# A new order for every engine: planner slots, distance and step in a kernel of a Fourier half and a state-space half

## The chip, the cores and the metric

The kernel runs on one core of a Trainium2 chip. Five engines work side by side: TensorE (PE; its weight loads are listed apart as PEld), VectorE (DVE), ScalarE (ACT), GpSimd (POOL) and SyncE (SP), which here only issues transfers. The metric is the device time of one execution in microseconds (us); lower is better.

## The reference

Two independent layers, whose outputs stand side by side. All values are float32.

```
# A: Fourier mixing, x is 2048 x 512
a = x @ dft_hid_re.T ;  b = x @ dft_hid_im.T
y = dft_seq_re @ a - dft_seq_im @ b

# B: a diagonal state-space layer, u is 2048 x 512, 128 states per channel
dt = exp(log_dt);  A = -exp(log_A_real) + 1j * A_imag
P  = exp((A * dt)[:, :, None] * arange(2048))
K  = 2 * real(sum over the states of C * dt * P)        # one filter of 2048 taps per channel
y  = irfft(rfft(u, 4096) * rfft(K, 4096))[:2048] + u * D_skip

out = concatenate([A, B])
```

## The kernel before

**The Fourier half** (class `Fnet`) multiplies by the sequence matrix first and by the hidden one afterwards. It works in twelve groups, eight of sixteen tiles ("s") and four of eight tiles ("p", which reads the sums of the s groups back from memory). Each float32 tile is split into a rounded part `hi` (ACT, L231) and the rest `lo` (DVE, L236), and one product is three matmuls (L380): hi times hi, hi times lo, lo times hi. Of the s tiles, those in `SOFTS` get their `lo` without DVE: two accumulating transfers from GpSimd's queue do it (L329, L334). The matmuls of one tile for one of four output columns are one request of 0.683 us to TensorE; they are the stream that TensorE works on whenever nothing else is due (urgency 5).

**The state-space half** (class `Ssm`) has these stages:
- `setup` and `setup_rest`: exponentials (`exp`, L505) and parameters (`params`, L561), once for the first 128 columns and once for the other 384.
- Sixteen chunks of 32 channels. `seed_args` (L654) makes angles and moduli, mostly on ACT; `seeds` their products; `tables1` and `tables2` build tables of powers by repeated complex multiplication on DVE (L623 `prod`, L632 `t`, L639, L646, L652).
- `taps` (L818): 128 short matmuls per chunk give the filter's taps. `stage1_k` (L867): the first step of the filter's transform, per two chunks, stored to `xk`.
- `stage1_u` (L922): the same for the input, in eight parts.
- Four quarters of the channels, each in four parts: loads of both spectra (L999), `product` (matmuls L1046, pointwise products on DVE L1030 and L1032, matmuls L1073), a store to `zs` (L1097), and then two `inverse` (L1167) or, for the last two quarters, `inverse2` (additions on DVE L1136 and L1138, matmuls L1145, output).

**The order is planned on the host.** Instructions are issued to each engine in the order in which a small simulation (class `Plan`) finishes choosing them; semaphores keep the data right whatever the order. A stage is a generator that yields requests: an engine, a price, perhaps an urgency of its own, and for TensorE the number of instructions. `Plan.run` (L171) takes the request with the smallest `key` (L149): first the step of time in which it could start, in steps of `GRAIN`; within one step the urgency, smaller first; then the start itself. All instructions that the code issues after a yield, up to the next one, have that place in the order, whatever engine they are for.

`Plan.step` (L103) moves a request later than its process's last one: by `HOP` where the engine changes, and by `RESULT` where a DVE operation follows a DVE operation whose result it needs (those that are marked `*APART` do not need it). Prices are `act(cols)` and `dve(cols, rate)`, (66 + cols/rate)/960 us for DVE. A request to TensorE also bears the planner's model of instruction fetching, in blocks of 256.

Urgencies: splits 0 (3 when the stream is ahead), seeds, taps, products of the first quarters and stores 1, tables 2 and 2.2, third-quarter products 3 (`LATE`), last-quarter products 1 (`LAST`), inverses of the last two quarters 2 (`AFTER`), the stream 5.

In several places the yields do not match the instructions behind them: `exp` asks for DVE where an ACT operation follows, `seed_args` asks for a DVE slot with no instruction behind it, and `params` issues some operations without a slot.

Of the kernel before, what the change touches and what calls it, by code (L numbers as in the profile page):

```python
# [51 lines left out]
    return [np.ascontiguousarray(a.astype(np.float32)) for a in (f1u, f1k, w2, ia, ib, ib2)]  # L52


HOP, RESULT, LATENCY = 0.3, 0.15, 3.3
STREAM = 5
GRAIN = 0.05
BLOCK, ASKS, LASTS = 256, 110, 400
ASKED, APART_BY, COMES = 2.0, 3.8, 2.4
APART = None, True  # L60
LATE = 1, 1, 3, 1
AFTER = 2
LAST = 1


# [24 lines left out]
class Plan:  # L90
# [12 lines left out]
    def step(self, p, value):  # L103
        self.now = p[0]
        while True:
            try:
                r = p[3].send(value)
            except StopIteration:
                return
            value = None  # L110
            if isinstance(r, Event):
                if r.time is None:
                    r.waiting.append(p)
                    return
                p[0] = max(p[0], r.time)
            elif isinstance(r, Sem):
                if not r.free:
                    r.waiting.append(p)
                    return
                p[0] = max(p[0], r.free.pop(0))  # L120
            else:
                if r[0] != p[5]:
                    p[0] += HOP
                elif r[0] == "dve" and len(r) < 4:
                    p[0] += RESULT
                p[4], p[5] = r, r[0]
                self.ready.append(p)
                return
            self.now = p[0]
# [19 lines left out]
    def key(self, p):  # L149
        engine, _, *urgency = p[4]  # L150
        start = max(p[0], self.free.get(engine, 0.0))
        if engine == "pe":
            start += self.fetched(p[4], start)[0]
        return int(start / GRAIN), urgency[0]() if urgency and urgency[0] else p[1], start, p[2]

# [34 lines left out]
def act(cols):  # L190
    return 0.09 + cols * 0.00085


def dve(cols, rate=1.0):
    return (66 + cols / rate) / 960
# [6 lines left out]
class Fnet:  # L202
# [117 lines left out]
                self.plan.spawn(self.load(src, None, self.m, i, self.m_ev[i]), urgency)  # L320

    def soft(self, i):
        return i[0] == "s" and (2 * i[1] + i[2], i[3]) in SOFTS

    def load_soft(self, src, i):

        hi, lo = (self.pool.tile([128, DM], F32R, name=m, bufs=DEPTH) for m in ("hi", "lo"))
        yield "pool", ISSUE
        self.nc.gpsimd.dma_start(hi, src)  # L329
        yield "dma", load(256)  # L330
        yield "act", act(512)
        self.nc.scalar.activation(lo, hi.bitcast(F32), AF.Copy, scale=-1.0)  # L332
        yield "pool", ISSUE
        self.nc.gpsimd.dma_start(lo, src, accum_op=OP.add)  # L334
# [106 lines left out]
class Ssm:  # L441
# [63 lines left out]
    def exp(self, x, k, f, p):  # L505

        n = math.prod(x.shape[1:])
        a, v = self.nc.scalar, self.nc.vector
        yield "dve", dve(n, 2)
        v.tensor_scalar(x, x, -87.0, 88.0, op0=OP.max, op1=OP.min)  # L510
        yield "dve", dve(n, 2)
        v.tensor_scalar(k, x, 1.0 / math.log(2.0), RND, op0=OP.mult, op1=OP.add)
        yield "dve", dve(n, 2)
        v.tensor_scalar(k, k, RND, None, op0=OP.subtract)
        yield "dve", dve(n)
        v.scalar_tensor_tensor(f, k, -LN2_HI, x, op0=OP.mult, op1=OP.add)
        yield "dve", dve(n)
        v.scalar_tensor_tensor(f, k, -LN2_LO, f, op0=OP.mult, op1=OP.add)
        yield "dve", dve(n, 2)
        a.activation(p, f, AF.Copy, scale=EXP[0])  # L520
        for c in EXP[1:]:
            yield "dve", dve(n)
            v.scalar_tensor_tensor(p, p, c, f, op0=OP.add, op1=OP.mult)
        yield "dve", dve(n)
        yield "dve", dve(n, 2)
        a.activation(f.bitcast(I32), k, AF.Copy, scale=2.0 ** 23, bias=127.0 * 2.0 ** 23)
        yield "dve", dve(n)
        v.scalar_tensor_tensor(x, p, 1.0, f, op0=OP.add, op1=OP.mult)
# [32 lines left out]
    def params(self, par, alpha, dt, k):  # L561

        a, v = self.nc.scalar, self.nc.vector
        n = par.shape[2]
        yield "dve", dve(n), *APART
        v.tensor_tensor(par[:, 0], alpha, dt, op=OP.mult)
        yield "dve", dve(n), *APART
        v.scalar_tensor_tensor(par[:, 1], par[:, 1], 1.0 / (2 * math.pi), dt, op0=OP.mult, op1=OP.mult)

        a.activation(k, par[:, 1], AF.Copy, scale=-1.0, bias=RND)  # L570
        yield "dve", dve(n), *APART
        v.tensor_tensor(par[:, 2], par[:, 2], dt, op=OP.mult)
        yield "dve", dve(n), *APART
        v.scalar_tensor_tensor(par[:, 3], par[:, 3], -1.0, dt, op0=OP.mult, op1=OP.mult)
        v.scalar_tensor_tensor(par[:, 1], k, RND, par[:, 1], op0=OP.subtract, op1=OP.add)
        v.tensor_scalar(par[:, 1], par[:, 1], 0.5, -0.5, op0=OP.min, op1=OP.max)

    def setup(self):
# [75 lines left out]
    def seed_args(self, ck, box, ev):  # L654

        a, v = self.nc.scalar, self.nc.vector
        if CHUNK * ck >= FIRST:
            yield from self.load_par(ck)
        par = self.par[ck]
        yield self.res  # L660
        s = self.tab.tile([128, 3, 11, CHUNK], F32, name="seed")
        args = s[:, 0:3:2]
        e, k, r = (s[:, n] for n in range(3))
        n = 11 * CHUNK
        yield "act", act(2 * n) + 4 * act(0)
        a.activation(args[:, :, 0], par[:, 0:2], AF.Copy)
        for j in (1, 2, 4, 8):
            a.activation(args[:, :, j:min(2 * j, 11)], args[:, :, 0:min(j, 11 - j)], AF.Copy, scale=2.0 ** j)
        yield "act", act(n)
        a.activation(k[:, 1:], r[:, 1:], AF.Copy, scale=-1.0, bias=RND)  # L670
        yield "dve", dve(n)
        v.scalar_tensor_tensor(r[:, 1:], k[:, 1:], RND, r[:, 1:], op0=OP.subtract, op1=OP.add)
        yield "dve", dve(n, 2)
        yield "act", act(n)
        a.activation(k, r, AF.Abs)
        yield "act", act(n) + 1.3
        a.activation(e, e, AF.Exp, scale=-1.0)
        yield "act", act(6 * CHUNK) + 1.4
        a.activation(r[:, 0:6], r[:, 0:6], AF.Sin, scale=TWO_PI)
        yield "act", act(5 * CHUNK)  # L680
        a.activation(r[:, 6:11], r[:, 6:11], AF.Sin, scale=-TWO_PI)
        yield "act", act(n)
        a.activation(k, k, AF.Sin, scale=-TWO_PI, bias=self.halfpi)
        box.append(s)
        self.plan.set(ev)
# [417 lines left out]
    def inverses(self, h):  # L1103
# [5 lines left out]
        for i in range(2):  # L1109
            yield b.zls  # L1110
            self.plan.spawn((self.inverse2 if h >= HALVED else self.inverse)(b, h, i, 16), 1 if h < 2 else AFTER)

# [67 lines left out]
CHUNK, FIRST, JOIN = 32, 128, 0  # L1180
HALVED = 2
RAWS, DEPTH, STAGED, AHEAD = 7, 4, 4, 3
ISSUE = 1.0
SOFTS = {(g, k) for g in range(1, 8) for k in (3, 7, 11, 15)}
BATCH = 2


# [72 lines left out]
```

## Time and profile before

| | |
|---|---|
| median of 3 runs | 576.67 us (574.18 to 576.96) |
| profiled execution | 576.01 us |
| its span, from the first to the last instruction | 574.2 us |
| granted TensorE clock, mean | 0.999 |
| PE busy / weight loads | 566.7 us (99%) / 432.7 us (75%) |
| DVE busy | 518.5 us (90%) |
| ACT busy | 374.9 us (65%) |
| DMA | 133.70 MB, 233 GB/s |

The span is what the trace covers; the time of the execution is 1.8 us longer. A matmul's row is longer than the time until the next matmul starts, since they are pipelined, so a busy share of 99% says that TensorE nearly always has something in flight, not that it can do no more. Waits are the idle time of an engine before an instruction, with the event that ended it. The chain that ended last is followed back from the last instruction through what released each step.

### The profile page before, as it was taken

The page shows a single profiled execution, that of the slowest core. Times are in us where ns is not written, and L with a number is a line of the kernel's source. Part 1 is how long each engine was busy: PE and PEld are TensorE (multiplying, and loading weights), DVE is VectorE, ACT ScalarE, POOL GpSimd, SP SyncE. Part 2 cuts the span into 40 slices and gives each one's busy share as a digit, 9 for nine tenths or more (in the row PEclk, how much of TensorE's full clock was granted, in tenths as well). Part 3 has the DMA queues.
Part 4 walks back from the last instruction along what each step waited for, and adds up shares of the span by engine and source line. Part 5 has one row for each costly group of instructions (what it writes and reads, how often), then busy time and mean ns, then how long its engine had stood idle before and what let it go on. Part 6 is the DMA issues. An engine that isn't in the chain of part 4 may idle for free.

```text
span 574.2 us, 15643 instructions
## 1 busy us (share of the span) xinstructions
PE 566.7 (99%) x6278; PEld 432.7 (75%) x6278; DVE 518.5 (90%) x909; ACT 374.9 (65%) x734; POOL 40.3 (7%) x60
## 2 busy tenths in 40 slices
PE   8999999999999999999999999999999999999997
PEld 6877777788877777778787777777687778776685
DVE  6999999999999999999999999999999999447732
ACT  5789766673778495858669586845588845355623
POOL 0000101100110000100101001001100000000000
PEclk9999999999999999999999999999999999999999
DMA  7999999987459767867697888569998896599994
GB/s 247 329 358 274 289 285 283 274 281 196 134 148 223 210 184 227 202 164 236 181 250 198 222 206 259 134 164 278 276 299 227 226 298 230 125 281 270 276 228 147
DMA packets 147976, 133.70 MB, mean 233 GB/s; under 512 B 47296, under 2 KB 107328, under 8 KB 147648
## 3 DMA queue, kind: packets, MB, share of 16 engines
q1 hardware_dynamic: 138976, 115.54, 67.1%
q0 software_dynamic: 8064, 14.68, 12.8%
q10 hardware_dynamic: 864, 2.49, 1.7%
q8 instruction: 49, 0.80, 0.6%
q14 instruction: 23, 0.19, 0.1%
HBM read 89.95 MB, written 42.73 MB: 231 GB/s over the span
## 4 chain that ended last, share of the span: by engine, by line
PE 88%; DVE 7%; issue 2%; ACT 1%; DMA 1%; DVEq 0%
PE acc L380 69%; PE f L1046 5%; PE f L818 5%; PE f L1073 3%; DVE prod L623 2%; DVE t L632 2%; PE f L867 1%; DVE lo L236 1%; PE f L1167 1%; PE f L922 1%; PE f L1145 1%; DMA out_yb<-zl 1%; DMA raw<-in_sT 1%; DVE zl L934 0%; DVE t L652 0%
## 5 line engine op out<-in xcount | busy, mean ns | idle before, releaser
L380 PE MATMUL acc<-hi,x_hi 128*128 128x512 f32 x640 | 258.2, 403 | 0.1
L380 PE MATMUL acc<-lo,x_hi 128*128 128x512 f32 x640 | 250.3, 391 | 0.0
L380 PE MATMUL acc<-hi,x_lo 128*128 128x512 f32 x640 | 249.7, 390 | 0.0
L623 DVE TENSOR_TENSOR prod<-t,cs 128x1024 f32<-128x1024 f32 (+4 forms) x192 | 163.5, 870 | 1.8 <-ACT t L740 0.6
L380 PEld LDWEIGHTS acc<-hi,x_hi 128*128 128x128 f32 x640 | 120.3, 188 | 49.0 <-issue 23.0
L380 PEld LDWEIGHTS acc<-hi,x_lo 128*128 128x128 f32 x640 | 120.4, 188 | 26.0
L380 PEld LDWEIGHTS acc<-lo,x_hi 128*128 128x128 f32 x640 | 120.5, 188 | 23.1 <-DVE lo L236 0.2
L231 ACT ACTIVATE hi<-raw 128x512 fp32r<-128x512 f32 x132 | 82.8, 629 | 71.5 <-PE acc L380 56.2
L236 DVE TENSOR_TENSOR lo<-raw,hi 128x512 fp32r<-128x512 f32 x132 | 90.6, 688 | 25.3 <-ACT hi L231 25.0
L632 DVE TENSOR_TENSOR t<-prod 128x512 f32<-128x512 f32 (+4 forms) x192 | 94.6, 515 | 1.0
L639 ACT ACTIVATE square<-t 128x256 f32<-128x256 f32 (+1 forms) x64 | 36.8, 575 | 26.3 <-DVE t L632 24.4
L334 POOL DMA_DIRECT2D lo<-in_sT x28 | 24.3, 869 | 206.9 <-ACT lo L332 64.4
L1025 ACT ACTIVATE uk<-f 128x1024 f32<-128x1024 f32 x32 | 31.1, 1018 | 10.8 <-PE f L1046 9.0
L401 ACT ACTIVATE y<-acc 128x512 f32<-128x512 f32 x47 | 28.0, 595 | 12.8 <-PE acc L380 12.7
L818 PEld LDWEIGHTS f<-t,t 128*32 128x32 f32 x2048 | 29.5, 110 | 6.8 <-issue 4.8
L818 PE MATMUL f<-t,t 128*32 128x64 f32 x2048 | 32.2, 220 | 0.9 <-issue 0.8
L329 POOL DMA_DIRECT2D hi<-in_sT x28 | 15.8, 566 | 193.8 <-PE acc L380 135.5
L1030 DVE TENSOR_TENSOR z<-uk 128x512 f32<-128x512 f32 x32 | 22.0, 687 | 4.4 <-ACT uk L1025 2.9
L1088 ACT ACTIVATE z<-f 128x512 f32<-128x512 f32 x32 | 17.7, 593 | 12.0 <-PE f L1073 12.0
L652 DVE TENSOR_TENSOR t<-square 128x128 f32<-128x128 f32 (+1 forms) x64 | 25.0, 390 | 0.0
L1046 PE MATMUL f<-xt,w 64*32 64x256 f32 x768 | 23.5, 379 | 0.0
L1032 DVE TENSOR_TENSOR uk<-uk 128x512 f32<-128x512 f32 x32 | 22.1, 691 | 0.9
(104 smaller groups left out, 497.8 us busy)
## 6 DMA issues: line engine op xcount, KB each, us to landing
raw<-in_sT SPq DMA_DIRECT2D x99, 256.0 KB, 5.2
p<-y SPq DMA_DIRECT2D x32, 256.0 KB, 3.7
xk<-xk_sb SPq DMA_DIRECT2D x32, 256.0 KB, 5.2
zs<-z SPq DMA_DIRECT2D x32, 256.0 KB, 3.8
raw<-p SPq DMA_DIRECT2D x32, 256.0 KB, 4.6
hi<-in_sT POOLq DMA_DIRECT2D x28, 256.0 KB, 4.7
lo<-in_sT POOLq DMA_DIRECT2D x28, 256.0 KB, 5.0
xt<-xu SPq DMA_DIRECT2D x24, 256.0 KB, 4.6
```

Source lines behind the costliest of these rows:

```text
L231: self.nc.scalar.activation(hi, src, AF.Copy)
L236: self.nc.vector.tensor_tensor(lo, src, hi.bitcast(F32), op=OP.subtract)
L334: self.nc.gpsimd.dma_start(lo, src, accum_op=OP.add)
L380: nc.tensor.matmul(acc[d], l[:, cols], r, start=k == 0 and n == 0, stop=k == len(items) - 1 and n == 2)
L401: self.nc.scalar.activation(y, ps, AF.Copy, scale=-1.0 if g[2] == 1 else 1.0)
L623: self.nc.vector.tensor_tensor(p.rearrange("p k d c m -> p k (d c) m"), src.rearrange("p d c l -> p (d c) l")[:, None, :, rows].to_broadca ...
L632: self.nc.vector.tensor_tensor(dst[:, :, :, rows], p[:, 0], p[:, 1, :, ::-1], op=OP.add)
L639: self.nc.scalar.activation(sq, t[:, :, :, m // 2:m], AF.Square)
L652: self.nc.vector.tensor_tensor(t[:, :, 0, m:2 * m:2], box[0][:, :, 0], box[0][:, :, 1], op=OP.subtract)
L818: nc.tensor.matmul(ps[32 * j:32 * j + 32, i], t1[:, d, c], t2[:, d, c], start=c == 0, stop=c == 1, tile_position=(0, 32 * j))
L1025: a.activation(uk[:, r].rearrange("p g c n d -> p g (c n d)"), p, AF.Copy)
L1046: nc.tensor.matmul(got[r][1][32 * xx:32 * xx + 32, g, 256 * c:256 * c + 256], self.w2[rows, 2 * q + r, xx, 32 * c:32 * c + 32], xt[rows].r ...
```

## The change

Only the planner's numbers and the slots that the stages ask for are changed. No operation, tile, buffer or transfer is added or taken away; all engines and queues get the same instructions in an order planned anew.

- `RESULT` 0.15 to 0.2, `GRAIN` 0.05 to 0.1, `AFTER` 2 to 1.
- A new `SLACK` of 0.1 us on top of `HOP` where a process goes from another engine to TensorE.
- `exp`: the two ACT operations get ACT slots, where there were one and two DVE slots.
- `params`: the ACT operation and two DVE operations get slots of their own.
- `seed_args`: two slots are shorter by 32 columns, and a DVE slot without an operation goes.
- `SOFTS` is written out as a list of 28 pairs, and `soft` asks for `SOFT`, groups 1 to 7, too.

```diff
-HOP, RESULT, LATENCY = 0.3, 0.15, 3.3
+HOP, RESULT, LATENCY = 0.3, 0.2, 3.3
 STREAM = 5
-GRAIN = 0.05
+SLACK = 0.1
+GRAIN = 0.1
...
-AFTER = 2
+AFTER = 1
...
                 if r[0] != p[5]:
-                    p[0] += HOP
+                    p[0] += HOP + (SLACK if r[0] == "pe" else 0.0)
...
     def soft(self, i):
-        return i[0] == "s" and (2 * i[1] + i[2], i[3]) in SOFTS
+        return i[0] == "s" and 2 * i[1] + i[2] in SOFT and (2 * i[1] + i[2], i[3]) in SOFTS
...
         v.scalar_tensor_tensor(f, k, -LN2_LO, f, op0=OP.mult, op1=OP.add)
-        yield "dve", dve(n, 2)
+        yield "act", act(n)
         a.activation(p, f, AF.Copy, scale=EXP[0])
...
-        yield "dve", dve(n)
-        yield "dve", dve(n, 2)
+        yield "act", act(n)
         a.activation(f.bitcast(I32), k, AF.Copy, scale=2.0 ** 23, bias=127.0 * 2.0 ** 23)
...
+        yield "act", act(n)
         a.activation(k, par[:, 1], AF.Copy, scale=-1.0, bias=RND)
...
+        yield "dve", dve(n), *APART
         v.scalar_tensor_tensor(par[:, 1], k, RND, par[:, 1], op0=OP.subtract, op1=OP.add)
+        yield "dve", dve(n, 2)
         v.tensor_scalar(par[:, 1], par[:, 1], 0.5, -0.5, op0=OP.min, op1=OP.max)
...
-        yield "act", act(n)
+        yield "act", act(n - CHUNK)
         a.activation(k[:, 1:], r[:, 1:], AF.Copy, scale=-1.0, bias=RND)
-        yield "dve", dve(n)
+        yield "dve", dve(n - CHUNK)
         v.scalar_tensor_tensor(r[:, 1:], k[:, 1:], RND, r[:, 1:], op0=OP.subtract, op1=OP.add)
-        yield "dve", dve(n, 2)
...
-ISSUE = 1.0
-SOFTS = {(g, k) for g in range(1, 8) for k in (3, 7, 11, 15)}
+ISSUE, SOFT = 1.0, range(1, 8)
+SOFTS = {(6, 15), (4, 3), (3, 7), (5, 7), (4, 15), (1, 3), (2, 11), (1, 15), (7, 7), (6, 11), (3, 3), (5, 3), (4, 11), (3, 15), (5, 15), (2, 7), (1, 11), (7, 3), (6, 7), (7, 15), (4, 7), (3, 11), (5, 11), (7, 11), (2, 3), (1, 7), (2, 15), (6, 3)}
```

## The prediction

> **What bounds the kernel now.** I read the page of the profile first (busy line, chain, groups), then the busy time by stage, then TensorE's own rows, because a matmul row lasts longer than the time until the next one starts and so the busy share of PE says little. The page, cut:
>
> ```profile
> span 574.2 us, 15643 instructions
> ...
> PE 566.7 (99%) x6278; PEld 432.7 (75%) x6278; DVE 518.5 (90%) x909; ACT 374.9 (65%) x734; POOL 40.3 (7%) x60
> ...
> q8 instruction: 49, 0.80, 0.6%
> ...
> PE 88%; DVE 7%; issue 2%; ACT 1%; DMA 1%; DVEq 0%
> ...
> L236 DVE TENSOR_TENSOR lo<-raw,hi 128x512 fp32r<-128x512 f32 x132 | 90.6, 688 | 25.3 <-ACT hi L231 25.0
> ```
>
> The chain is 88% PE and 7% DVE. The view of stretches (columns: length, then busy us of PE, PEld, DVE, ACT, POOL with counts, granted clock, DMA share, GB/s) shows that DVE is full as well until about 480 us, and not after:
>
> ```profile
> 40.00:420.00 380.00, 378.46 (x4266) 289.88 (x4265) 375.83 (x660) 262.36 (x530) 38.65 (x54) 1.00 0.81 223
> 440.00:480.00 40.00, 40.00 (x432) 31.10 (x432) 39.97 (x69) 26.08 (x51) 0.87 (x1) 1.00 0.92 260
> 480.00:560.00 80.00, 80.00 (x966) 59.60 (x965) 47.34 (x75) 36.41 (x58) 0.00 (x0) 1.00 0.84 235
> ```
>
> DVE has 375.83 of 380 us and then 39.97 of 40. So two chains run side by side: TensorE's total work, and the state-space half's way through DVE. In the timeline of TensorE (start, length, instruction) one sees how tightly it runs:
>
> ```profile
> 57.16 0.39 PE L380 MATMUL acc<-hi,x_hi 128*128 128x512 f32 x1
> ...
> 58.30 0.39 PE L380 MATMUL acc<-hi,x_lo 128*128 128x512 f32 x1
> 58.61 1.11 PE L922 MATMUL f<-xt,f1u 32*64 32x512 f32 x16
> 59.66 0.50 PE L380 MATMUL acc<-hi,x_hi 128*128 128x512 f32 x1
> 59.99 0.40 PE L380 MATMUL acc<-lo,x_hi 128*128 128x512 f32 x1
> ```
>
> Five steps from 57.16 to 58.30 are 0.228 us each, under the 0.39 us of a row: the stream of the Fourier half never pauses. Leaving it for a group costs 58.61 - 58.30 = 0.31, coming back 59.99 - 59.66 = 0.33, so one round trip costs about 0.08 + 0.10 = 0.18 us, and an undisturbed L922 group takes 59.66 - 58.61 = 1.05 us. A new order can't shorten any of the matmuls; on TensorE it can win the places where a group stands waiting for an input, and a few round trips. These are those places, in the weight loads' timeline (in brackets the idle time before, and what ended it):
>
> ```profile
> 47.47 0.21 PEld L922 LDWEIGHTS f<-xt,f1u 32*64 32x64 f32 x8 [0.35 <-issue]
> 49.55 0.19 PEld L380 LDWEIGHTS acc<-hi,x_hi 128*128 128x128 f32 x1 [0.81 <-ACT lo L332]
> ...
> 77.47 0.21 PEld L922 LDWEIGHTS f<-xt,f1u 32*64 32x64 f32 x8 [0.35 <-ACT hi L231]
> 79.34 0.19 PEld L380 LDWEIGHTS acc<-hi,x_hi 128*128 128x128 f32 x1 [0.81 <-issue]
> 83.15 0.45 PEld L818 LDWEIGHTS f<-t,t 128*32 128x32 f32 x26 [0.54 <-ACT hi L231]
> ...
> 163.09 0.70 PEld L867 LDWEIGHTS f<-ks,f1k 32*64 32x64 f32 x32 [0.99 <-issue]
> ...
> 231.60 0.19 PEld L1073 LDWEIGHTS f<-uk,ia 32*64 32x64 f32 x4 [0.35 <-issue]
> 233.31 0.19 PEld L380 LDWEIGHTS acc<-hi,x_hi 128*128 128x128 f32 x1 [0.39 <-issue]
> ...
> 403.53 1.71 PEld L818 LDWEIGHTS f<-t,t 128*32 128x32 f32 x118 [0.36 <-issue]
> 406.17 0.25 PEld L818 LDWEIGHTS f<-t,t 128*32 128x32 f32 x10 [0.92 <-issue]
> 406.51 0.19 PEld L380 LDWEIGHTS acc<-hi,x_hi 128*128 128x128 f32 x1
> ```
>
> and in the chain that ended last (start, length, what), which also has the undisturbed lengths of L1073 and L818 and the tail:
>
> ```profile
> 191.20 1.24 PE f L1073 x32
> ...
> 252.86 1.05 PE f L1073 x32
> ...
> 353.35 1.51 PE f L1073 x32
> ...
> 427.26 1.92 PE f L818 x128
> ...
> 485.80 1.92 PE f L818 x128
> ...
> 564.56 1.12 PE f L1145 x64
> ...
> 566.82 3.17 DMA out_yb<-zl
> 569.99 0.60 ACT y L396
> ```
>
> Stalls, each against its undisturbed form: L922 at 47.47 took 2.08, so 1.03 too long; at 77.47 it took 1.87, 0.82 too long. A group is normally entered after 0.35 us without a weight load; 83.15 and 163.09 show 0.54 and 0.99, so 0.19 and 0.64. L1073 needs 1.05 and took 1.24, 1.71 (231.60 to 233.31) and 1.51: 0.19, 0.66, 0.46. L818 needs 1.92 and took 2.98 from 403.53 to 406.51: 1.06. Sum 5.05 us. With all of it gone the span would be 574.2 - 5.05 = 569.15 us. That is the most that waits on TensorE can give.
>
> The tail: the last tables' group is at 485.80, the last inverse ends at 564.56 + 1.12 = 565.68, and TensorE then still works on its stream until 569.99 - so the state-space chain has 4.3 us to spare. Earlier gains nothing; later by more than 4.3 us costs one for one.
>
> **The change, part by part.** No instruction is added or removed on the chip; the only difference is the order in which each engine and queue gets the same instructions.
>
> *The list in SOFTS* names the same 28 tiles as before and SOFT holds all seven groups: nothing, either way.
>
> *Slots.* The planner's price of a DVE operation is (66 + columns)/960 us, half the columns at double rate. Taken out: sixteen slots of 352 columns at double rate in the seeds, 16 x 0.252 = 4.03 us, and 32 columns from sixteen others, 0.53; in the two exponentials (260 and 384 columns) 0.20 + 0.27 for the first mislabelled slot and 0.54 + 0.74 for the second pair. Put in: two DVE slots each for 128 and 384 columns in the parameters, 0.20 + 0.47 + 0.14 + 0.27. Net 6.31 - 1.08 = 5.2 us less planned DVE time. ACT gains about 2 us of slots in place of them. On the chip this is worth nothing directly. But the phantom slots made the plan later than the chip, which was distance between DVE's results and TensorE's groups; that cover goes. Over some 440 us of full DVE it is 1.2%, and it was spread over the sixteen chunks at 0.25 us each. Ends: a group that relied on it waits up to 0.25 us more (16 x 0.25 = 4 us lost), or none does. I take 0, since the next part gives back 0.1 us and most groups stand behind several microseconds of stream.
>
> *SLACK and GRAIN.* Every request to TensorE by a process that comes from another engine moves 0.1 us later. That covers the 0.19 us stalls at 83.15 and 191.20 by half or more, and only 0.1 of each larger one: eight stalls x 0.1 = 0.8 us as a sure lower end of what the distance itself gives. The coarser step, 0.1 us in place of 0.05, lets a more urgent operation win although it is ready up to 0.1 us later; on TensorE the extra 0.05 cancels part of the distance, on DVE it can leave idle time (third rival). Beyond that, the whole list is drawn anew, and the large stalls (1.03, 0.82, 0.64, 0.66, 0.46, 1.06: 4.67 us) will not stand where they stand. Ends: all gone, -4.67; as many and as many again elsewhere, +4.67. I take half gone, -2.3, nearer to the good end because 1.03, 0.82 and 0.64 sit before 165 us where processes from ACT and DMA hand over, and distance is what they lack. With the two small ones (0.4): -2.7 us.
>
> *RESULT from 0.15 to 0.2.* The DVE timeline has a pair where the second needs the first, and a pair that does not:
>
> ```profile
> 52.72 0.69 DVE L934 TENSOR_TENSOR zl<-f,zl 128x512 f32<-128x512 f32 x1
> 53.44 0.69 DVE L936 TENSOR_TENSOR zl<-f,zl 128x512 f32<-128x512 f32 x1
> ...
> 56.58 0.69 DVE L934 TENSOR_TENSOR z<-f,z 128x512 f32<-128x512 f32 x1
> 57.18 0.69 DVE L236 TENSOR_TENSOR lo<-raw,hi 128x512 fp32r<-128x512 f32 x1
> ```
>
> 0.72 against 0.60 us start to start: the true distance is 0.12, and both settings are above it. Where another operation stands between, 0.12 us of DVE is saved; if none does, nothing changes. DVE time before 480 us only moves the state-space chain, which is off the end by 4.3 us: 0.
>
> *AFTER from 2 to 1.* The inverses of the last two quarters now tie with the last products. Their eight additions (512 columns, 0.60 us each by the pair above) can go ahead of the last product: up to 4.8 us on the state-space chain, 0.5 beyond the 4.3 to spare. Nearest row: DVE is busy 47.34 of 80 us there, so I take 0.
>
> *Queues.* SP's transfers are issued in planned order too, each behind the wait of the one before:
>
> ```profile
> SPq L1097 <- ACT z L1088: 49.9, 12, 10.5
> ```
>
> One store of z held the queue for 10.5 us. A load of a later stream tile behind such a wait is late by as much; the buffers of seven raw tiles cover it now, since the stream itself shows no gap. I take 0; if the cover fails once, it costs some microseconds (fourth rival).
>
> *Round trips:* TensorE comes back to the stream some 55 times:
>
> ```profile
> PEld acc L380 <- issue: 23.0, 55, 0.8
> ```
>
> Five pairs of groups merged or split are 5 x 0.18 = 0.9 us either way; I take 0.
>
> Sum: 574.2 - 2.7 = 571.5 us of span. The profiled execution took 576.01, 1.8 more than its span, and the median of the three runs is 576.67, 0.7 above it: 571.5 + 1.8 + 0.7 = 574.0. The distance given to each group makes the draw better than an even one by another 0.8; I settle on 573.2, a gain of 0.6%.
>
> **The rivals.**
> *No change* (the new order doesn't do what it says): the phantom slots' cover goes, 0.1 us of distance comes, and stalls of the same total stand elsewhere. For it: six of the eight stalls are larger than 0.1 us. Against: distance alone gives 0.8. Time 576.7, give or take 2.5.
>
> *More than the waits:* below 569.15 + 1.8 + 0.7 = 571.7 only by merged round trips, say 570.8, or if TensorE's rows hide more. The Trainium skill, in "Perfetto Trace Analysis", section "Identifying the Most-Contended Engine", says that the busy share of matmuls is no measure of what is left and that of weight loads is; that share is 75% here, which would leave far more to win. The rows decide otherwise: weights of 0.19 us every 0.228 us with no gap in the stream.
>
> *Slower, the state-space chain comes late.* In a step of 0.1 us the splits (L236, urgency 0) and products (1) go before the tables (2 and 2.2), and DVE waits for them. At most 132 splits x 0.1 = 13.2 us, at half a step 6.6. It decides at 4.3: 6.6 would cost 2.3 and eat the gain (no change), 13.2 would cost 8.9: 576.7 + 8.9 - 2.7 = 582.9. For it: DVE is full until 480 us, with nothing to make it up. Against: the old step already paid half of this, and 5.2 us of phantom slots no longer push the tables back. The Trainium skill, in "TensorE: Matmul & The Clock Gate", Part 1, says that TensorE falls to half its clock after about 3.4 us of idling; so a starved tail would cost more than the wait itself. The clock column is 1.00 throughout, so no stretch here shows it.
>
> *Slower, new stalls on TensorE:* 49 blocks of instructions are fetched (queue 8), and the 1.06 us stall at 403.53 is next to one:
>
> ```profile
> q8 instruction: 1, 0.02, 0.7%
> ```
>
> (the view of transfers, 400 to 408 us). Where blocks end inside groups of short matmuls is drawn anew. Five more such stalls are 5.3 us: 576.7 + 5.3 = 582.0 without the gain; a stream tile held back on SP costs as much.
>
> **How the numbers follow.** About 0.5%, 2.9 us, is what a measurement of this kernel tells from no change: faster is under 573.8, slower over 579.6. The forecast gets 0.53 with a range of its own from 570.8 to 575.5, of which 0.45 lies below 573.8 and 0.08 within; no change 0.19, within; more than the waits 0.03, faster; the late chain 0.14 and new stalls 0.11, slower. So 0.48, 0.27 and 0.25. The range begins at 569.8 (all waits and some ten round trips gone) and goes up to 580.5, which takes in the lighter half of the two slow cases; about 0.15 lies beyond.
>
> **What would show it.** Right: L818, L1073 and L922 groups at 1.92, 1.05 and 1.05 us with one or two exceptions, the last L818 not after 490 us, and the last matmuls on the stream. Wrong: stalls that sum to 5 us or more in the weight loads' timeline (no change or new stalls, told apart by their places: at block fetches, behind L1097 on SP, or at DVE); or a last L818 after 490 us and a gap of TensorE before L1073 or L1145 in the tail (the late chain). If stalls shrink and the span doesn't, the round trips have grown.

## The result and the profile after

| | before | after |
|---|---|---|
| median | 575.76 us (574.18 to 576.96, 20 runs) | 577.41 us (574.95 to 579.45, 20 runs) |
| ratio to before, with its 95% interval | 1 | 1.0026 (1.0015 to 1.0038) |
| standard deviation of the runs | 0.74 us | 1.19 us |
| profiled execution, its span | 576.01, 574.2 us | 577.63, 575.8 us |
| last group of taps starts | 485.80 us | 489.79 us |
| last inverse ends | 565.68 us | 568.41 us |
| last instruction of ACT starts | 569.99 us | 571.43 us |

The change cost 0.26%, 1.65 us: less than the 0.5% that the prediction set as the bound of what can be told, and on the other side of no change than forecast. The page of the changed kernel, cut (span; busy time of the engines; the chain that ended last):

```profile
span 575.8 us, 15643 instructions
...
PE 566.7 (98%) x6278; PEld 432.8 (75%) x6278; DVE 518.6 (90%) x909; ACT 374.0 (65%) x734; POOL 40.2 (7%) x60
...
PE 81%; DVE 10%; ACT 4%; issue 2%; DMA 2%; SPq 0%; DVEq 0%; ACTq 0%
```

Busy times and counts of every engine are those of before within 0.9 us: the work costs what it did, and what grew is the time between the instructions. The same stretches as before (length, then busy us of PE, PEld, DVE, ACT, POOL with counts, granted clock, DMA share, GB/s):

```profile
40.00:420.00 380.00, 377.09 (x4194) 290.56 (x4179) 371.15 (x647) 257.37 (x524) 38.43 (x54) 1.00 0.80 220
440.00:480.00 40.00, 39.90 (x458) 32.09 (x464) 39.83 (x71) 23.91 (x47) 0.00 (x0) 1.00 0.67 200
480.00:560.00 80.00, 79.94 (x1118) 56.86 (x1103) 50.95 (x81) 39.96 (x62) 0.00 (x0) 1.00 0.94 259
```

From 40 to 420 us PE is busy 1.4 us less and DVE 4.7 us less. Most of what DVE lacks there stands behind 480 us (50.95 against 47.34), and with it more transfers: 259 against 235 GB/s. The new order runs the state-space half later.

Two views of TensorE in the changed kernel. First the weight loads' timeline (start, length, instruction, in brackets the idle time before and what ended it):

```profile
94.42 1.86 PEld L820 LDWEIGHTS f<-t,t 128*32 128x32 f32 x128 [0.89 <-ACT zl L934]
...
118.93 0.67 PEld L869 LDWEIGHTS f<-ks,f1k 32*64 32x64 f32 x32 [0.58 <-DVE ks L843]
...
361.05 0.19 PEld L381 LDWEIGHTS acc<-hi,x_hi 128*128 128x128 f32 x1 [0.52 <-issue]
```

then the timeline of the matmuls:

```profile
192.85 1.99 PE L820 MATMUL f<-t,t 128*32 128x64 f32 x128
...
198.32 0.39 PE L381 MATMUL acc<-hi,x_hi 128*128 128x512 f32 x1 [1.20 <-issue]
```

A group is entered after 0.35 us without a weight load, so the taps at 94.42 (line L818 before, L820 now) waited 0.54 us for their input and the first transform step at 118.93 0.23. The stream stopped for 1.20 us at 198.32 though nothing that it needs was late: a block of instructions (queue 8) was fetched from 196.10 to 197.06, and the stream went on 1.26 us after that.

To sum such places over the whole kernel I set the start of each request to TensorE on the chip against the planner's own start for it. The difference is called the lag below; a jump of the lag is a wait that the plan doesn't have. From 15 us to the end the lag grows by 3.5 us in the profile of before and by 6.2 us in that of after. The plan itself ends 0.9 us earlier (567.0 against 567.9), which leaves 2.7 - 0.9 = 1.8 us; the spans differ by 1.6. In after the jumps over 0.2 us stand at 70.9 (0.22), 94 (0.65), 119 (0.29), 160 (0.45), 168 (0.54), 198 (1.37), 281 (0.30), 343 (0.53), 361 (0.48), 416 (0.27), 445 (0.26) and 513 to 515 us (0.33, 0.24). Two of them are stalls of before that went along with their group: the first taps (0.30 at 83, now 0.65 at 94) and the second transform step of the filter (0.76 at 163, now 0.54 at 168). The other old stalls went, and a larger sum came.

The tail in the chain that ended last:

```profile
489.79 1.93 PE f L820 x128
...
508.55 0.69 SPq L1001
...
509.29 3.58 DMA x_lo<-xk
...
512.92 1.93 PE f L1048 x56
...
567.32 1.09 PE f L1147 x64
568.41 3.00 PE acc L381 x12
```

The last taps start 4.0 us later than before. The last quarter's spectrum loads (L1001) are issued behind stores of z on SP, land at 512.87, and the product at 512.92 waits for them. Behind the last inverse 3.00 us of stream are left, where there were 4.3.

### The profile page after: what moved, and what is told of

The parts are those of the page before. It is cut to its first block, busy times and chain, and to the rows that moved or that the text cites. A ratio compares the mean times of both kernels' runs of the same rounds, so it can differ in the third digit from the quotient of the medians.

```text
span 575.8 us, 15643 instructions
## 1 busy us (share of the span) xinstructions
PE 566.7 (98%) x6278; PEld 432.8 (75%) x6278; DVE 518.6 (90%) x909; ACT 374.0 (65%) x734; POOL 40.2 (7%) x60
## 4 chain that ended last, share of the span: by engine, by line
PE 81%; DVE 10%; ACT 4%; issue 2%; DMA 2%; SPq 0%; DVEq 0%; ACTq 0%
PE acc L381 64%; PE f L1048 5%; PE f L820 4%; DVE prod L626 4%; PE f L1075 3%; DVE t L635 2%; DVE lo L237 2%; PE f L1169 1%; PE f L869 1%; PE f L924 1%; ACT hi L232 1%; PE f L1147 1%; DMA x_lo<-xk 1%; DMA p<-y 1%; DMA raw<-in_sT 1%
## 5 line engine op out<-in xcount | busy, mean ns | idle before, releaser
L820 PEld LDWEIGHTS f<-t,t 128*32 128x32 f32 x2048 | 29.5, 110 | 6.5 <-issue 4.0
L820 PE MATMUL f<-t,t 128*32 128x64 f32 x2048 | 32.2, 220 | 0.7 <-DVE zl L938 0.5
```

The costliest lines, as they stand in the source:

```text
L820: nc.tensor.matmul(ps[32 * j:32 * j + 32, i], t1[:, d, c], t2[:, d, c], start=c == 0, stop=c == 1, tile_position=(0, 32 * j))
```

## The experiments

Most kernels here are other settings of the same planner, so what the planner itself expects stands beside the time: the planned end of TensorE's last request, which is worked out on the host while the kernel is built. "New slots" are those of the change, "old slots" those of before. All times are medians, ratios are to runs of the kernel before on the same chip. The expectations of e12, e15 and e16 give the planned end of all engines instead, which is 0.8 or 0.9 us later (568.7 for before, 567.8 for after).

| run | slots | planned end | time, us (range, runs) | ratio (95%) | time less plan |
|---|---|---|---|---|---|
| before | old | 567.9 | 575.76 | 1 | 7.9 |
| after | new | 567.0 | 577.41 | 1.0026 (1.0015 to 1.0038) | 10.4 |
| e1_before_nudge | old | 584.0 | 593.63 (592.80 to 595.22, 4) | 1.0313 (1.0289 to 1.0337) | 9.6 |
| e2_after_nudge | new | 575.0 | 585.97 (585.34 to 587.53, 4) | 1.0181 (1.0158 to 1.0203) | 11.0 |
| e3_slots_only | new | 577.9 | 585.35 (584.03 to 586.12, 4) | 1.0162 (1.0136 to 1.0187) | 7.5 |
| e4_numbers_only | old | 572.2 | 580.32 (580.18 to 580.99, 4) | 1.0081 (1.0063 to 1.0098) | 8.1 |
| e5_after_shift | new | 567.0 | 577.14 (575.50 to 579.41, 12) | 1.0022 (1.0009 to 1.0035) | 10.1 |
| e6_before_fetch | old | 567.7 | 576.56 (576.00 to 577.84, 11) | 1.0010 (1.0000 to 1.0021) | 8.9 |
| e7_after_slack0 | new | 575.0 | 586.06 (585.38 to 586.74, 2) | 1.0177 (1.0158 to 1.0195) | 11.1 |
| e8_after_slack4 | new | 582.9 | 595.24 (595.03 to 595.46, 2) | 1.0336 (1.0318 to 1.0354) | 12.3 |
| e9_z_on_pool | new | 567.0 | 577.02 (575.14 to 579.19, 12) | 1.0012 (0.9993 to 1.0030) | 10.0 |
| e10_after_again | new | 567.0 | 576.22 (575.46 to 579.25, 8) | 1.0013 (0.9992 to 1.0035) | 9.2 |
| e11_after_again | new | 567.0 | 577.04 (576.00 to 579.21, 8) | 1.0013 (0.9996 to 1.0030) | 10.0 |
| e12_far_blocks | new | 567.0 | 580.19 (577.85 to 582.10, 7) | 1.0067 (1.0043 to 1.0091) | 13.2 |
| e13_before_again | old | 567.9 | 575.53 (574.33 to 576.26, 8) | 0.9988 (0.9977 to 0.9999) | 7.6 |
| e14_before_again | old | 567.9 | 575.82 (575.43 to 576.84, 8) | 1.0004 (0.9991 to 1.0016) | 7.9 |
| e15_draw_a | new | 566.7 | 577.04 (575.51 to 579.06, 10) | 1.0019 (1.0001 to 1.0036) | 10.3 |
| e16_draw_b | new | 566.8 | 582.90 (581.76 to 584.26, 4) | 1.0108 (1.0091 to 1.0126) | 16.1 |
| e17_old_slots_a | old | 566.8 | 577.93 (575.41 to 581.06, 12) | 1.0039 (1.0021 to 1.0056) | 11.1 |
| e18_old_slots_b | old | 566.6 | 576.75 (573.66 to 580.32, 12) | 1.0017 (0.9997 to 1.0037) | 10.2 |

### Has a part of the change an effect of its own?

My theory after the result: no; each setting draws another order, and what counts is the draw ("the draw"). The rival: slots and numbers each have an effect, and these add up ("the parts"). Two kernels change nothing but the planner's price of a stream request, by a thousandth of a microsecond; the same edit in before (e1) and in after (e2):

```diff
-                        yield "pe", 0.683, None, 6
+                        yield "pe", 0.684, None, 6
```

> The kernel before with one number of the planner moved by a thousandth of a microsecond: the price of a stream request 0.684 in place of 0.683; nothing else, and the same instructions. Theory 'the draw' (the order comes out of many close races, so that any small change of a number gives another order, and before and after are two low draws): far from before, 592 to 595 us, because the planner's own end for this order is 584.0 against 567.9 for before, and the chip ended 8 to 11 us behind the planner's end in the two kernels seen. Rival 'the parts' (each part of the change has an effect of its own): a thousandth of a microsecond is no part, so 575 to 577 us, as before.

> The changed kernel with the price of a stream request 0.684 in place of 0.683. The draw: 583 to 586 us (planner's own end 575.0 against 567.0 for after). The parts: 577 to 578 us, as after.

Two do half of the change each. e3 has the new slots with the numbers of before; e4 has the numbers with the old slots:

```diff
-HOP, RESULT, LATENCY = 0.3, 0.15, 3.3
+HOP, RESULT, LATENCY = 0.3, 0.2, 3.3
-GRAIN = 0.05
+SLACK = 0.1
+GRAIN = 0.1
-AFTER = 2
+AFTER = 1
-                    p[0] += HOP
+                    p[0] += HOP + (SLACK if r[0] == "pe" else 0.0)
```

> Only the slots of the change (exponentials, parameters, seeds), with RESULT 0.15, no SLACK, GRAIN 0.05 and AFTER 2 as before. The draw: 586 to 589 us (planner's own end 577.9), and the two halves of the change do not add up to the whole. The parts: the phantom slots' cover is lost and nothing given for it, so a few more waits on TensorE, 576 to 580 us, and this difference plus that of the numbers alone is the 1.65 us of the whole change.

> Only the numbers of the change (RESULT 0.2, SLACK 0.1, GRAIN 0.1, AFTER 1), with the slots of before. The draw: 580 to 583 us (planner's own end 572.2). The parts: distance without loss of cover, 573 to 576 us.

And two turn the one number that is new, `SLACK`, in the changed kernel: to 0 (e7) and to 0.4 (e8).

```diff
-SLACK = 0.1
+SLACK = 0.0
...
-SLACK = 0.1
+SLACK = 0.4
```

> The changed kernel with SLACK 0. The draw: 583 to 586 us (planner's own end 575.0), whatever SLACK is for. The parts (distance keeps groups from waiting): a little worse than the changed kernel, 577.5 to 580, with more waits of groups for DVE and ACT before 480 us.

> The changed kernel with SLACK 0.4 us, four times the distance. The draw: 591 to 594 us (planner's own end 582.9). The parts: 574 to 577. Apart from the total, what distance does for the waits: before 480 us TensorE's groups should lose less against the plan than with SLACK 0, if distance covers late inputs at all; what is left would be blocks of instructions.

Measured: the thousandth of a microsecond costs before 593.63 - 575.66 = 18.0 us (575.66 is the median of before on that chip) and after 585.97 - 577.41 = 8.6 us. Slots alone cost 9.7 and numbers alone 4.7 us against the same 575.66; together they cost 1.65. Less distance (e7) is slower than after by 8.7 us, and more of it (e8) by 17.8. No sum and no direction is left: the rival falls. All six end 7.5 to 12.3 us after their plan, as before and after do; e3, e7 and e8 lie 0.1 to 1.2 us outside the range that the draw gave them.

What makes most of these draws slow is the tail. In all six TensorE's last work is an inverse, with no stream left behind it. TensorE's waits by line waited for (total us, times, longest), in e1, then in e8:

```profile
PE f L1145 <- DVE zsum L1136: 6.1, 2, 3.3
```

```profile
PE f L1147 <- DVE zsum L1138: 10.1, 1, 10.1
```

In e2 and e7 the same row has 4.1 us (longest 3.1) and 3.9 us. The state-space half comes late, the stream is used up, and TensorE stands before the last inverses. That is the prediction's third rival, past its point of 4.3 us. In e3 and e4 this row has 0.6 us at most; in e3 the stream itself stands for its own splits (2.06 us up to 523.20), and so it does in e1 (3.57 us up to 529.37). The end of e1 in stretches of 4 us, columns as above:

```profile
570.00:574.00 4.00, 4.00 (x20) 3.25 (x18) 0.00 (x0) 1.79 (x3) 0.00 (x0) 1.00 1.10 285
574.00:578.00 4.00, 0.91 (x15) 0.33 (x21) 1.60 (x3) 0.60 (x1) 0.00 (x0) 0.99 1.02 257
578.00:582.00 4.00, 2.17 (x60) 1.26 (x48) 1.08 (x2) 1.09 (x2) 0.00 (x0) 0.50 0.96 285
582.00:586.00 4.00, 2.20 (x52) 1.32 (x58) 2.67 (x4) 0.00 (x0) 0.00 (x0) 0.50 0.50 135
```

The stream's last matmul ends at 574.34 (573.95 and 0.39 in the timeline), TensorE then stands for 2.86 us and gets only a few short matmuls at 577.20, and at 578 us the granted clock falls to 0.50 and stays there. The Trainium skill, in "TensorE: Matmul & The Clock Gate", Part 1, has TensorE at half its clock after an idle window of about 3.4 us. This trace agrees in the half; its gap is rather shorter, with a thinly used 0.8 us behind it. After the stop of 3.57 us up to 529.37 the clock is at 0.50 too, from 530.16 to 533.57 us.

The planner says how rare good draws are, in a count on the host that no run on the chip bears out. With the new slots and some 7,000 random sets of its numbers, its planned end (the latest of all engines) has a median of 578.9 us, and one in twenty lies under 569.2; with the old slots the median is 581.3. Before (568.7 by this measure) and after (567.8) are both among the lowest in twenty. The median of such a count hangs on how far the numbers are varied, the place of the two kernels far less. I had compared two lucky draws as if a redraw could only help the one.

### Are the remaining waits due to block fetches?

The second theory ("late blocks"): between good draws the difference is where block ends fall, and moving them gains the 1.2 us of 198 us and its like. e5 keeps the order of after and puts 64 more instructions (weight loads and matmuls) into the warm-up, into a tile that nobody reads, so that each block ends elsewhere:

```diff
-        for n in range(3):
-            self.nc.tensor.matmul(ps[:, :256], z[:, :128], z[:, 256:], start=n == 0, stop=n == 2)
+        self.nc.tensor.matmul(ps[:, :256], z[:, :128], z[:, 256:], start=True, stop=True)
+        w = z.bitcast(mybir.dt.bfloat16)
+        for n in range(36):
+            self.nc.tensor.matmul(ps[:32, :32], w[:32, :32], w[:32, 64:96], start=True, stop=True)
```

> The changed kernel's own order, with 64 more instructions on TensorE ahead of the first real matmul (the three warm-up matmuls become one and 36 tiny ones into a tile that nobody reads), so that every block of 256 fetched instructions ends 64 instructions earlier in the work; the planner is not told. Theory 'late blocks' (most of what the changed kernel loses against its own plan is TensorE waiting for instruction blocks): the four jumps at 198.3, 281.6, 361.3 and 416.2 us of the changed kernel (1.4, 0.3, 0.5, 0.3 us) are gone or stand elsewhere, next to other fetches; since the order was drawn for the old block ends and not for these, the sum need not fall: 575.0 to 580. Rival 'late inputs' (these waits are for data from DVE, ACT or transfers): the four jumps stay where they are, 577 to 578.5.

e6 lets the planner of before count a block as there 3.6 us after it is asked for, where it had 2.4; its order keeps groups of short matmuls away from block ends:

```diff
-ASKED, APART_BY, COMES = 2.0, 3.8, 2.4
+ASKED, APART_BY, COMES = 2.0, 3.8, 3.6
```

> The kernel before, planned with 3.6 in place of 2.4 us from asking for a block of instructions to having it; everything else as before, and the planner's own end at 567.7 against 567.9. The order is that of before up to 212 us. Late blocks: no wait next to a fetch after 212 us, where before loses 0.9 us at 406.5 and 0.4 at 354.8; its lag on the plan falls by 1.3 us: 574.0 to 575.0. Late inputs: lag as before or a new draw of it, 575.5 to 578.

In e5's profile the jumps at 198, 281, 361 and 416 us are gone; one at 342 stays, and small ones at 146 and 425 us are new. Those at 361 and 416 count, since they stand in every profile of the unaltered kernel (below), which the one at 198 doesn't. In e6's the waits of before near 355 and 406 us are gone, but L1073 waits 1.23 us at 228.5 with no fetch near, and 0.85 at 468: there it stops in the middle and goes on at 469.34, 1.55 us after a fetch that ended at 467.79. So the expectation that no wait stands next to a fetch missed, and the lag fell by 0.3 us, not by 1.3. The waits at 361 and 416 do belong to the fetches, but neither median is lower by more than the runs vary: 577.14 in place of 577.41, and 576.56 in place of 575.97 on that chip. So the place of the blocks explains single waits and not the difference.

### Is it the loads held on SP, or just the spread of runs?

e9 has the order of after and issues the stores of the third quarter's z from GpSimd, so that the spectrum loads don't stand behind them:

```diff
-            self.nc.sync.dma_start(view[2 * q + r], t[:, r])
+            (self.nc.gpsimd if h == 2 else self.nc.sync).dma_start(view[2 * q + r], t[:, r])
```

> The changed kernel's own order, but the third quarter's stores of z (eight transfers) are issued by GpSimd, whose queue is idle then, in place of SP. In the changed kernel the last of these stores hold SP from 505.7 to 508.5 us, the loads of the last quarter's filter spectrum stand behind them, and TensorE waits 0.67 us for x_lo at 513. Theory 'held loads' (this wait on SP's queue is a good part of the 1.65 us that the changed kernel loses, and of the larger spread of its runs): no wait of TensorE for x_lo near 513, time 575.7 to 576.7, and a spread of the runs nearer to that of before. Rival 'spread out' (the loss is many small waits all along): 576.9 to 577.6.

The wait at 513 us is gone, and the lag from 480 to 560 us grows by 0.29 in place of 0.96. But e10, the unaltered kernel profiled again (below), has no wait there either and grows by 0.38, so this profile doesn't show that the edit did it. The median is 577.02 (0.9993 to 1.0030 of before), in the rival's range and 0.39 under that of after, and the two intervals overlap: not shown to be worth anything. (Its profile lost 2 us at the start, where the stream's matmuls start every 0.43 us up to 10.3 us, and in after only up to 6.0.)

Since single profiles carried such weight, the unchanged kernels were profiled again, after twice and before twice:

> The changed kernel once more, unaltered, for a second profile. Its time 575 to 579. Held loads: its excess over its fastest runs stands at the last quarter's first group (near 513 us) and differs between the profiles there. Spread out: the same places wait in both profiles, and the total differs by small amounts everywhere.

> The changed kernel a third time, unaltered, for a third profile, with the same expectation as the second.

> The kernel before, unaltered, for a second profile, to set beside the three profiles of the changed kernel. 575 to 577 us. If the changed kernel's loss is its own places (TensorE waiting at 94, 160, 361 and 416 us in each of its profiles), the kernel before shows its own set of places again, with a smaller sum after the first ten microseconds: about 3.5 us against the plan, where the changed kernel had 4.6 to 7.3. If the loss is chance of the runs, the sums overlap.

> The kernel before, unaltered, a third profile, with the same expectation as the second.

The repeats of after come out at 1.0013 twice (0.9992 to 1.0035, 0.9996 to 1.0030), those of before at 0.9988 (0.9977 to 0.9999) and 1.0004. So a kernel differs from itself by about 0.1%, and the loss that is left to explain is 0.1 to 0.3%. Growth of the lag, us:

| profile | 15 to 480 us | 480 to 560 us |
|---|---|---|
| before, e13, e14 | 3.3, 2.7, 3.3 | 0.08, 0.09, 0.09 |
| after, e10, e11 | 5.2, 4.2, 4.1 | 0.96, 0.38, 3.04 |

Each stretch holds about half of the 2.7 us on average: 4.5 - 3.1 = 1.4 and 1.46 - 0.09 = 1.4. The waits at 94, 119, 160, 168, 343, 361 and 416 us are in all profiles of after; the largest, 1.37 at 198, is in one of three. The tail of before never loses anything, and that of after loses more or less in each execution. e10 and e11 are the same kernel on the same chip, at 576.22 and 579.21 us. A quarter's z is read back from memory by transfers of SP and ACT. SP's first read for one of the inverses, issued at 530.75 us in e10 and at 533.27 in e11 (count, KB each, us from issue to landing), e10, then e11:

```profile
zl<-zs SPq DMA_DIRECT2D x1, 512.0 KB, 9.2
```

```profile
zl<-zs SPq DMA_DIRECT2D x1, 512.0 KB, 11.7
```

The first addition on DVE and the inverse on PE, in e10:

```profile
541.99 0.69 DVE L1138 TENSOR_TENSOR zsum<-zl 128x512 f32<-128x512 f32 x1 [1.32 <-DMA zl<-zs]
```

```profile
544.79 0.30 PE L1147 MATMUL f<-zsum,ib 64*32 64x128 f32 x2
...
545.99 0.50 PE L381 MATMUL acc<-hi,x_hi 128*128 128x512 f32 x1
```

And in e11:

```profile
544.98 0.69 DVE L1138 TENSOR_TENSOR zsum<-zl 128x512 f32<-128x512 f32 x1 [1.88 <-DMA zl<-zs]
```

```profile
546.04 0.41 PE L1147 MATMUL f<-zsum,ib 64*32 64x128 f32 x4
...
547.66 0.41 PE L1147 MATMUL f<-zsum,ib 64*32 64x128 f32 x4 [0.55 <-DVE zsum L1138]
548.38 0.30 PE L1147 MATMUL f<-zl,ib 64*32 64x128 f32 x2 [0.32 <-DVE zl L1140]
...
548.97 0.50 PE L381 MATMUL acc<-hi,x_hi 128*128 128x512 f32 x1
```

In e11 SP issues the read 2.5 us later, behind two stores of z and a load that take it longer, and the read is under way 2.5 us longer. It lands at 544.97, and the first addition waits for it and starts 3.0 us later than in e10 (where it waits for a read of ACT's). TensorE takes up the inverse before the second pair of additions is done, and needs 548.97 - 546.04 = 2.93 us for it in place of 545.99 - 544.79 = 1.20. That one group holds 1.73 of the 3.0 us between the two executions. Why the read takes 9.2 us in one and 11.7 in the other can't be seen; a long read alone costs nothing, since in before SP's reads in the tail take 9.4 us (median of four) and the lag doesn't grow. From 480 to 565 us, before first, after second (packets and bytes; stores of z):

```profile
DMA packets 21404, 18.95 MB, mean 223 GB/s; under 512 B 5184, under 2 KB 16788, under 8 KB 21392
...
zs<-z SPq DMA_DIRECT2D x10, 256.0 KB, 3.9
```

```profile
DMA packets 28983, 21.77 MB, mean 256 GB/s; under 512 B 5499, under 2 KB 24955, under 8 KB 28971
...
zs<-z SPq DMA_DIRECT2D x14, 256.0 KB, 5.9
```

The new order puts four more of the stores, and 2.8 MB more in all, into the tail, and the median store lands 2.0 us later (in the repeats 5.1 and 6.4 us after against 4.5 and 4.3 before). That goes with the loss but isn't enough to cause it: e18 moves 21.59 MB there and lost 0.27, and e17 moves 18.68 MB and lost 3.9 (below).

### Is there a better draw?

If the planner's end and blocks that come later were enough, orders that are planned as early as after's and keep away from block ends would be faster than both kernels. Three have the new slots:

The first, e12:

```diff
-HOP, RESULT, LATENCY = 0.3, 0.2, 3.3
+HOP, RESULT, LATENCY = 0.278, 0.1969, 3.3
-SLACK = 0.1
-GRAIN = 0.1
+SLACK = 0.1429
+GRAIN = 0.045
-ASKED, APART_BY, COMES = 2.0, 3.8, 2.4
+ASKED, APART_BY, COMES = 2.0, 3.8, 3.6
-AFTER = 1
+AFTER = 2
```

The second, e15, and the third, e16, which leaves `COMES` at 2.4; both have `AFTER` 2 too:

```diff
+HOP, RESULT, LATENCY = 0.2919, 0.1582, 3.3
+SLACK = 0.1775
+GRAIN = 0.0718
+ASKED, APART_BY, COMES = 2.0, 3.8, 3.6
```

```diff
+HOP, RESULT, LATENCY = 0.28, 0.12, 3.3
+SLACK = 0.15
+GRAIN = 0.03
```

> The slots of the change with other numbers (HOP 0.278, RESULT 0.1969, SLACK 0.143, GRAIN 0.045, blocks of instructions 3.6 us after asking): one draw out of some 3400 orders planned on the host, taken because the planner's own end is low (567.8, as low as before's 567.9), because blocks are given more time, and because its last tables' group comes at 481.1 and its last inverse at 558.9 by the plan, 3 us earlier than in before. The draw: as before, 575.0 to 576.5. Late blocks and held loads together: less lag on the plan, 573.5 to 575.0, faster than both kernels. The parts (more distance, but the finer step): no statement closer than 574 to 578.

> Another low draw of the planner with the slots of the change (HOP 0.2919, RESULT 0.1582, SLACK 0.1775, GRAIN 0.0718, blocks of instructions 3.6 us after asking). Planner's own end 567.5, last tables' group planned at 482.8, last inverse at 562.7. The draw: planner's end plus 7.5 to 11 us as in the orders run so far, 575.0 to 578.5; nothing says where in it. Late blocks: at the low end, 575 to 576, with no wait next to a fetch.

> Another low draw with the slots of the change (HOP 0.28, RESULT 0.12, SLACK 0.15, GRAIN 0.03, blocks 2.4 us after asking as in both kernels). Planner's own end 567.6. The draw: 575.1 to 578.6. Late blocks: at the high end, 577 to 578.6, with waits next to fetches.

Two have the old slots, in case the slots are what holds the lag down ("cover"), and `AFTER` 2; e17 and e18:

```diff
+HOP, RESULT, LATENCY = 0.2778, 0.1758, 3.3
+SLACK = 0.0315
+GRAIN = 0.0543
+ASKED, APART_BY, COMES = 2.0, 3.8, 3.0
```

```diff
+HOP, RESULT, LATENCY = 0.2798, 0.1958, 3.3
+SLACK = 0.0191
+GRAIN = 0.0692
+ASKED, APART_BY, COMES = 2.0, 3.8, 2.6
```

> The slots of before, with numbers that draw an order that is low by the planner: TensorE's last request ends at 566.8 by the plan (before 567.9, after 567.0), the last inverse is planned at 558.7. Theory 'cover' (the phantom DVE slots of before make the plan later than the chip and so keep it from falling behind; orders with the old slots fell 2.7 to 3.3 us behind the plan between 15 and 480 us, orders with the new ones 2.8 to 11.4): 3 us behind, as before, so 574.2 to 575.3 us, faster than both. The draw alone, without cover: anywhere from 574.5 to 582.

> As the run before, another draw with the slots of before (HOP 0.2798, RESULT 0.1958, SLACK 0.019, GRAIN 0.069, blocks 2.6 us after asking): TensorE's last request ends at 566.6 by the plan. Cover: 574.0 to 575.2 us. The draw alone: 574.5 to 582.

None is faster than before; e15, e17 and e18 lie in the range that the draw gave them, e12 and e16 above everything expected. The five plans end within 0.4 us of each other and the times spread over 6.2 us: below one per cent the planner doesn't rank orders. e16's lag grows by 11.4 us from 15 to 480 us, with no one large wait: the largest jumps are 1.35 and 1.34 us, at 406 and 414 us.

On the cover: from 15 to 480 us the lag grows by 1.8 to 3.3 us in all eight profiles with old slots (before three times, e1, e4, e6, e17, e18), and by 2.8 to 5.2 us in eleven of the twelve with new slots (e16: 11.4). That points to about 1 us that the phantom slots had covered, but the ranges overlap, and the expectation that the times follow was wrong for e17 and e18. What e17 won there it lost in its tail. Its transfers from 526 to 542 us, and DVE:

```profile
zl<-zs SPq DMA_DIRECT2D x2, 512.0 KB, 13.4
```

```profile
539.24 0.69 DVE L1137 TENSOR_TENSOR zsum<-zl 128x512 f32<-128x512 f32 x1 [7.53 <-DMA zl<-zs]
```

It is the same place as in e11: the read of z, here 13.4 us long, then additions, then an inverse that takes 2.1 us too long.

Room in the tail doesn't prevent it. In e12 and e17 the last taps start at 483.71 and 484.00 us, earlier than in before (485.80), and 7.05 and 7.08 us of stream stand behind the last inverse, where before has 4.3; yet their lag grows by 2.1 and 3.9 us from 480 to 560 us, and that of before by 0.1.

## Why the prediction was wrong

**The step that failed** is the redraw: "I take half gone, -2.3", with -0.4 for the small stalls and another -0.8 for the distance. Six of the eight stalls did go. But I priced only what could go and let what comes with a new order stand at zero, although the text had the other end, "as many and as many again elsewhere, +4.67". The lag against the plan grew by 6.2 us in place of 3.5, +2.7, where -3.5 stood in the sum. The -0.8 was also counted twice, since the same distance was already the reason for taking half and not less. Nor is it a sure lower end: of the eight stalls those at 353.35 and 403.53 us stand next to block fetches (ended at 352.94 and 404.79), which distance isn't for. (All eight are larger than 0.1 us; the first rival says six.) The draws of e1 to e4, e7 and e8 show why a draw of this planner can't be leaned towards gain: all six orders are slower by 0.8 to 3.4%, and e6, which is before's order up to 212 us, is no faster. Beside it the base of the sum was off: it set the median 0.7 us above the profiled execution after three runs, and over twenty it lies 0.25 below.

**Distance** isn't shown to gain anything here. The two stalls that stayed are waits of a group for its input, which `SLACK` is for; the one at the first taps grew from 0.30 to 0.65 us. The times of e7 and e8 show no order by its size. Their lag up to 480 us does, a little: it grows by 4.6 us without distance (e7), 4.1 to 5.2 with 0.1 (after) and 3.2 with 0.4 (e8), as e8's expectation had it; but that is one profile each of three different orders, and e8's plan ends 15.9 us later than after's.

**Slots**, taken as 0 between 0 and 4 us lost: within the ends, about 1 us lost by the lag, not settled.

**The late state-space chain**: its place and its deciding point were right. The last taps came 4.0 us later and didn't decide; in e1, e2, e7 and e8 the chain was later than the stream could cover, and they end 8.6 us and more behind before or after. Its sign, the last taps after 490 us, was not: in e1 they start at 482.95, earlier than in before. What I missed is that the margin isn't all that counts in the tail: TensorE waits at products and inverses there (0.4 to 3.0 us) with 3.0 us of stream left. The larger traffic goes with these waits, but what causes them stays open: e12 and e17 have an earlier chain and more room than before, and lose 2.1 and 3.9 us there.

**Queues**, taken as 0: the spectrum loads did stand behind stores of z on SP, and the product waited for them, in two profiles of three; taking that away (e9) changed the median by no more than the runs vary.

**Block fetches** (fourth rival): right in kind, with a 1.37 us wait at 198 us in one profile of three and waits of 0.3 to 1.0 us at 361 and 416 us in all three, but before has such waits too (0.92 us at 406.51), and moving them had no effect on the median (e5).

**What held**: `SOFTS` and `AFTER` nothing (planned with `AFTER` 2, the changed kernel has the identical order on all engines); round trips the same, 56 rows "acc <- issue" for 55; matmuls unchanged; `RESULT` wasn't isolated, since any change of it is a draw. The rival "no change", 576.7 give or take 2.5, with "stalls of the same total stand elsewhere", is nearest to what came, and it should have been the likeliest.

## What to carry to other kernels

Where a static order comes out of a list planner, treat a change to its numbers as a new draw: nudge an unrelated price by a thousandth first, and see how far the time moves. Price what a new order brings as high as what it removes, and if the present order is a selected one, higher. Waits that a profile shows go when the order changes, and others come; below one per cent nothing tried here (planned end, block ends, slots, room in the tail) told how many. So look for the transfer whose landing sets a group, read its time by the single issue and not as a median over a window, and compare several profiles before you explain a difference under 1%.

## What the chip showed that was not expected

- One kernel, the same order, on one chip: the same read of z landed 9.2 us after its issue in one execution and 11.7 in another, and 1.73 of the 3.0 us between them are one group behind it. Before spreads by 0.74 us (standard deviation), after by 1.19, e18 by 1.87.
- After a block fetch the stream went on 1.26 us after the transfer's end (198.32), and in before the taps at 406.17 went on 1.38 us after a block that was fetched from 403.85 to 404.79. It is 1.55 us in e6 (469.34, fetch ended at 467.79) and 1.53 in e12 (310.66, 309.13). A block that has landed isn't yet a block that runs.
- Once TensorE had stood for 2.86 us in the tail of e1 the clock went to 0.50 up to the end of the kernel, and the matmuls of the last inverses took 405 and 414 ns each in place of 273 and 274 in before.
- Some groups take too long with no fetch in sight and no wait that the profile names: L1073 in before at 231.60, 1.71 us in place of 1.05, has no block fetched in the nine us before it. That stays open, and so does what makes the reads in the tail slow in one execution and not in the next.
